# Linear attention, then a noisy top-2 mixture of experts: two key decays issued later, and another order of work at the border to expert 0

## The chip, the cores and the metric

One core of a Trainium2 chip runs the whole kernel in one launch. The metric is the device time of a run in microseconds (us), from start to end; lower is better. The engines are named as the profile names them: PE (matrix products and transposes), ACT (activations and copies), DVE (vector operations), POOL (GpSimd, which also issues indirect DMAs), SP (DMA issues).

## The reference

The first part is linear attention with a decay per head (B 4, H 8, S 768, D 64), the second a mixture of 8 experts with noisy top-2 routing over 3072 tokens of width 512 (hidden width 1024). Cut to what matters:

```python
for b in range(nb):                                   # attention
    intra = einsum('bhic,bhjc->bhij', qb, kb) * Dmask[None]
    intra = einsum('bhij,bhjd->bhid', intra, vb)
    inter = einsum('bhid,bhde->bhie', qb * lam_pow[None], kv_state)
    out[:, :, sl] = intra + inter
    kb_dec = kb * rev_pow[None]
    kv_state = lam_block * kv_state + einsum('bhsd,bhse->bhde', kb_dec, vb)
noisy_logits = x @ w_gate + log1p(exp(x @ w_noise)) * noise     # x: the attention's output
top2 = argpartition(-noisy_logits, 2, axis=1)[:, :2]            # softmax over the two
for e in range(E):
    for k in range(2):
        h = maximum(x[mask] @ w1[e], 0.0)
        out[mask] += top2_w[mask, k, None] * (h @ w2[e])
```

## The kernel before

**Attention** runs in 12 stages `t` (loop from L937) of two chunks of 128 positions each, over all 8 heads. A stage has, in this order: the gate's products of the stage before (`products`, L416), the turning of that stage's output into rows (`turn_x`, L428), the transposes of the next stage's keys and queries (L312, L325), the state update (`kv`, L400), the decayed keys of the stage after next (`kdecay(t + 2)`, L340, 8 ACT operations), the stage's own sums (`intra`, `inter(t, 0)`, L368), the copy of the two accumulators to memory on ACT (`evac_o`, L388), the logits of the stage before (L447), the scores of the next stage (`scores`, L355 on PE, L358 on DVE), and the second half of `inter`. An engine runs its own instructions in the order in which this code records them; there is no other scheduler. The accumulators `pO` and `pKV` exist once, so the second half of `inter` for the next stage can't start before `evac_o` has read them. Keys arrive by a DMA on SP's queue, which also carries the weight loads of expert 0; a load whose buffer is still read waits there, and what stands behind it waits too.

**Routing** is cut into three groups of chunks (8, 8 and 8). For each group a generator records DVE steps one by one, whenever `advance(n)` is called: `gate` (L457 to L498: logits to noisy top-2, last result `ob`), `weights`, `count` (PE, L532 to L537: how many tokens stand before each one), then `route` (DVE, L548 to L572: positions, and the one-hot tables `hot` and `rest`), and after a break called "step" 24 small products that find expert 0's tokens (L583) and the DVE chain behind them (L586 to L612). `finish(n)` drives a group to its end. The lists of tokens per expert go to DRAM by scatters on POOL (L622, one of about 1 us for each chunk and choice; `scatter` issues them at once, `paced` one by one, each behind a one-element copy L670 that waits for the named tile). `gather_rows` (L813) fetches token rows by indirect DMA.

**The border** (L992 to L1016) is what stands between the last stage and expert 0's loop: `products(11)`, the transposes of the first two gathered tiles (`trans_rows`, L822 on PE, L824 on ACT, L825 on DVE), `logits(11)`, the first two of the eight column blocks f of expert 0 (`mm1`, 12 products each, L860; `head`), and their evacuation (`evac1`, L866 on ACT, L870 on DVE). PE's results rotate through 4 buffers `pS`, which `mm1`, `turn_x` and `trans_rows` share, so the block f = 2 needs the buffer of `head[0]`.

**Expert 0** (L1018 on) runs in three parts of 2, 2 and 3 tiles: the first layer (8 blocks f, L860), then for each tile the second layer (`gemm2`, 24 products, L898). Tiles 2 and 3 come from the second group, tiles 4 to 6 from the third. The third part ends with the reading of the scattered lists (`load_rec`), the gathers of expert 1's rows and their transposes (L822). Weights are split into a high part (ACT, L771) and a low part (L775, a difference of two tensors in SBUF, on DVE or POOL).

Of the kernel before, what the change touches and what calls it, by code (L numbers as in the profile page):

```python
# [56 lines left out]
MAXOV = 40  # L57
MAXT = 24
FILLA, FILLB, FILLC = {4: 24, 5: 24, 6: 20, 7: 20, 8: 19, 9: 19, NST - 1: 24}, 2, 4
FILL1, FILL2 = 4, 9  # L60
LOADS = {2: [(1, 0)], 3: [(1, 1)], 4: [(1, 2)], 5: [(1, 3)], 9: [(2, 0), (2, 1)], 10: [(2, 2)], 11: [(2, 3)]}
HIGH = {4: [(1, 0)], 5: [(1, 1)], 6: [(1, 2)], 7: [(1, 3)], 10: [(2, 0), (2, 1)]}
LOW = {5: [(1, 0)], 6: [(1, 1)], 7: [(1, 2)], 10: [(2, 0)]}
ZEROS = {11: 8}
MID = 16
X1 = ((), (), (), (), (0, 1), (2, 3, 4), (5, 6))
WARM = (10, 1, 1)
# [20 lines left out]
def sub(ap, offset, dims):  # L88
    return bass.AP(tensor=ap.tensor, offset=ap.offset + offset, ap=dims)
# [27 lines left out]
def kernel(  # L117
# [216 lines left out]
    def kdecay(u):  # L334
        if u >= NST:
            return
        KD[u] = aw.tile([128, 2, H, D], FT, name="kd", bufs=1)
        if u > 1:
            for h in range(H):
                nc.scalar.activation(KD[u][:, :, h, :], KT[u][:, :, h, :], AF.Copy, scale=kdc[:, h, :])  # L340
            return
        for a in range(2):
            kd, kt = [x[u][:, a].rearrange("p (h s) d -> p s h d", s=2) for x in (KD, KT)]
            nc.gpsimd.tensor_mul(kd, kt, kdc.rearrange("p (h s) d -> p s h d", s=2).to_broadcast([128, 2, HP, D]))
# [40 lines left out]
    def evac_o(u):  # L385
        XO[u] = aw.tile([128, 2 * DB * C], FT, name="xo", bufs=1).rearrange("p (a d i) -> p a d i", a=2, d=DB)
        for a in range(2):
            nc.scalar.activation(XO[u][:, a], PO[u][a], AF.Copy)  # L388
# [23 lines left out]
    def products(u):  # L412

        p = psum.tile([128, 2, C], FT, name="pR")
        for d in range(DB):
            nc.tensor.matmul(p[d * 32:(d + 1) * 32], wgn[:, d, :], XO[u][:, :, d, :], start=True, stop=True)  # L416
        XP[u] = aw.tile([128, 2, C], FT, name="xp", bufs=1)
        nc.scalar.activation(XP[u], p, AF.Copy)
# [3 lines left out]
    def turn_x(u):  # L422

        XC[u] = aw.tile([128, 2, DB, C], FT, name="xc")
        for a in range(2):
            p = bank()
            for d in range(DB):
                nc.tensor.transpose(p[:, d, :], XO[u][:, a, d, :], identf)  # L428
            nc.scalar.activation(XC[u][:, a], p, AF.Copy)

    def store_x(u):

        queue = nc.gpsimd if u < NST - 4 else nc.sync
        queue.dma_start(x_tok[2 * u * C:2 * (u + 1) * C, :].rearrange("(a p) m -> p a m", a=2),
                          XC[u].rearrange("p a d i -> p a (d i)"))
# [232 lines left out]
    def paced(n, tile):  # L668
        if scatters:
            nc.gpsimd.tensor_copy(spacer, tile[0:1, 0:1])  # L670
            scatter(n)
# [101 lines left out]
    def split_low(which, e, j, half=None, low=nc.vector):  # L773
        st, hi, lo = split_parts(which, e, j, half)
        low.tensor_tensor(lo, st, hi.bitcast(FT), op=SUB)  # L775
# [42 lines left out]
    def trans_rows(t, n):  # L818

        p = psum.tile([128, DB, n], FT, name="pS", bufs=4)  # L820
        for d in range(DB):
            nc.tensor.transpose(p[:, d, :], XG[t][:n, d * 128:(d + 1) * 128], identf[:n, :n])  # L822
        hi, lo = [xt(i, slice(t * TS, t * TS + n)) for i in range(2)]
        nc.scalar.activation(hi, p, AF.Copy)  # L824
        nc.vector.tensor_tensor(lo, p, hi.bitcast(FT), op=SUB)  # L825
# [111 lines left out]
    for t in range(NST):  # L937
        u = t + 1
        if t:
            products(t - 1)  # L940
            turn_x(t - 1)
            if t == 8:
                split_low(1, 0, 3, low=nc.gpsimd)
        if u < NST:
            trans_k(u)
        load(t + 3, "kt")
        if u < NST:
            trans_q(u)
        load(t + 3, "qt")
        if u < NST:  # L950
            kv(u)
        if t:
            store_x(t - 1)
            paced(1, XC[t - 1][:, 1, 0, :])
        kdecay(t + 2)
        if u == NST:
            scatter(1)
        if u == NST:
            logits(t - 1)
        intra(t)  # L960
        load(t + 3, "vt")
        inter(t, 0)
        evac_o(t)
        paced(1, XO[t][:, 1, 0, :])
        if t and u < NST:
            logits(t - 1)
        if 2 * t in GB[1:]:
            if 2 * t > GB[1]:
                finish(GB.index(2 * t) - 2, False)
            jobs.append(routing(GB.index(2 * t) - 1))  # L970
        advance(FILLB)
        if u < NST:
            scores(u)
            inter(u, 1)
        for which, j in HIGH.get(t, []):
            split_high(which, 0, j)
        if u < NST:
            if LOW.get(t):
                nc.gpsimd.tensor_copy(spacer, AT[u][0][0:1, 0, 0, 0, 0:1])
            for which, j in LOW.get(t, []):  # L980
                split_low(which, 0, j, low=nc.gpsimd)
            paced(1, AT[u][1][:, 1, 0, 0, :])
        advance(FILLA.get(t, 18))
        for which, j in LOADS.get(t, []):
            load_w(which, 0, j)
        zero_out(ZEROS.get(t, 0))
        if t == 2:
            turn_noise()
        if t == 4:
            for i in range(4):  # L990
                nc.sync.dma_start(sub(lst, i * 128 * LI * RW, [[LI * RW, 128], [1, LI * RW]]), linit)
    products(NST - 1)  # L992
    for j in range(2):
        trans_rows(j, TS)
    logits(NST - 1)
    head = [mm1(0, 0, PARTS0[0], 0)]
    turn_x(NST - 1)
    store_x(NST - 1)
    head.append(mm1(0, 0, PARTS0[0], 1))
    att.close()  # L1000
    hp = ctx.enter_context(tc.tile_pool(name="hp", bufs=1, reuse_waits="tile"))
    HT.append(hp.tile([128, FB, 2 * CAP], FR, name="ht"))
    for t in range(NT):
        if t >= len(XG):
            XG.append(hp.tile([128, DM], FT, name=f"xg{t}"))
        PV.append(hp.tile([128, DM], FT, name=f"pv{t}"))
    split_low(2, 0, 1)
    for f in range(2):
        evac1(0, 0, PARTS0[0], f, head[f])
    scatter(sum(job[0] == 0 for job in scatters))  # L1010
    load_rec(0, 0)
    finish(1, False)
    for t in range(2, 4):
        gather_rows(0, t, GB[2] * C)
    scatter(1)
    jobs.append(routing(NG - 1))  # L1016

    for i, (t0, n) in enumerate(parts(0)):  # L1018
        for f in range(FB):
            if i or f >= 2:  # L1020
                gemm1(0, t0, n, f)
            if i == 0:
                if 1 <= f < 5:
                    split_w(2, 0, 2 + (f > 2), (f - 1) % 2)
                if f == 2:
                    nc.scalar.activation(XG[6], zero, AF.Copy)
                advance(FILL1)
            if i == 1 and f < 4:
                advance(FILL2)
                if f == 3:  # L1030
                    finish(2, False)
            if i or f >= 2:
                paced(1 + (i == 2), ht(0, 0, f, columns(0, t0, n)).bitcast(FT))
            if i == 1 and f == 2:
                load_rec(0, 1)
            if i == 2 and f == 2:
                load_rec(1, 0)
                load_rec(0, 2)
                load_rec(0, 3)
                for j in range(1, 3):  # L1040
                    load_rec(1, j)
                for t in range(NT):
                    gather_rows(1, t)
            if i == 2 and f >= 4:
                for j in X1[f - 4]:
                    trans_rows(j, size(1, j))
        if i == 0:
            zero_out(NTOK // 128)
            advance(50)
        if i == 1:  # L1050
            which_expert(1, nc.sync)
            which_list(1, nc.sync)
            for j in range(4):
                load_w(1, 1, j)
        if i == 2:
            for t in range(t0):
                scatter_out(0, t, PV[t])
        for t in range(t0, t0 + n):
            if i < 2:
                paced(3, PV[t - 1] if t > t0 else ht(0, 0, FB - 1, columns(0, t0, n)).bitcast(FT))  # L1060
            gemm2(0, t)
            if t == 0:
                advance(50)
            for j in {0: (2, 3), 2: (4, 5, 6)}.get(t, ()):
                trans_rows(j, size(0, j))
            if i == 2:
                scatter_out(0, t, PV[t][:size(0, t), :])
            if i == 2:
                for j in range((0, 2, 4)[t - t0], (2, 4, 4)[t - t0]):
                    split_w(1, 1, j)  # L1070
                    load_w(2, 1, j)
                for j in X1[t]:
                    trans_rows(j, size(1, j))
# [180 lines left out]
```

## Time and profile before

| | before |
|---|---|
| median of 3 runs | 722.18 us (721.09 to 722.67) |
| the profiled execution (its span; the slowest core is the only one) | 732.3 us |
| PE busy | 705.6 us (96%) |
| DVE / ACT / POOL busy | 356.6 / 237.9 / 291.0 us (49 / 32 / 40%) |
| mean granted TensorE clock | 0.983 |
| chain that ended last, by engine | PE 74%; issue 6%; DVE 6%; DMA 6%; SPq 2%; ACT 2%; POOL 2% |
| HBM | read 87.15 MB, written 35.55 MB, 168 GB/s over the span |

The profiled execution is a run of its own beside the three, 10.1 us longer than their median. The page's first part gives each engine's busy time; the second cuts the span into 40 slices, and its clock row shows three slices at 0.8, all others at 0.9 (the slices are 18.3 us long; those at 0.8 begin at 0, 92 and 146 us); the fourth follows the chain that ended last back through its waits. Line numbers are those of the kernel before; in the changed kernel the lines behind L60 stand one or more lower.

### The profile page before, as it was taken

What the parts mean: (1) busy time and instruction counts of PE and PEld (TensorE: products, weight loads), DVE (VectorE), ACT (ScalarE), POOL (GpSimd) and SP (SyncE); (2) the same over time, 40 slices, a digit from 0 to 9 for tenths busy, and PEclk for the clock granted to TensorE, in tenths of its full rate; (3) what the DMA queues carried; (4) which work ended last, traced back from release to release, by engine and by line L of the source; (5) the groups of instructions that cost most, each with busy time, mean ns of one, the idle gap of its engine ahead of it and who ended that gap; (6) DMA issues with size and microseconds to landing.
All of it is one profiled execution on the core that took longest, in us unless ns stands there. A gap on an engine that the chain in (4) does not pass through costs nothing.

```text
span 732.3 us, 13486 instructions
## 1 busy us (share of the span) xinstructions
PE 705.6 (96%) x4909; PEld 602.5 (82%) x4909; DVE 356.6 (49%) x808; ACT 237.9 (32%) x451; POOL 291.0 (40%) x454
## 2 busy tenths in 40 slices
PE   7999989798998999999999999999999999999996
PEld 5888878697896798798879887988888898889885
DVE  6446948677424556464436443634453444435211
ACT  1677756331121423042214230423132332214100
POOL 6110545567847354524163406233412433221311
PEclk8999989989999999999999999999999999999999
DMA  9999998673516556856365637565465556540211
GB/s 204 216 234 228 244 232 216 184 255 78 120 19 217 186 161 187 256 151 187 122 231 161 188 101 248 153 187 194 145 176 159 192 184 188 165 147 14 79 43 38
DMA packets 137658, 122.50 MB, mean 167 GB/s; under 512 B 87642, under 2 KB 106458, under 8 KB 137588
## 3 DMA queue, kind: packets, MB, share of 16 engines
q1 hardware_dynamic: 122660, 80.50, 41.2%
q0 software_dynamic: 14512, 40.57, 17.5%
q8 instruction: 40, 0.66, 0.4%
q10 hardware_dynamic: 416, 0.53, 0.2%
q14 instruction: 30, 0.25, 0.1%
HBM read 87.15 MB, written 35.55 MB: 168 GB/s over the span
## 4 chain that ended last, share of the span: by engine, by line
PE 74%; issue 6%; DVE 6%; DMA 6%; SPq 2%; ACT 2%; POOL 2%; another core or an unknown queue 1%; POOLq 0%; ACTq 0%; DVEq 0%
PE pS L860 34%; PE pKV L898 14%; PE pO L898 13%; PE pS L355 2%; SPq L153 2%; DMA kt<-in_k_dram 2%; PE pKV L368 2%; PE pO L903 2%; PE pO L368 1%; PE pS L428 1%; DMA out_dram<-ot,rec 1%; PE pKV L903 1%; ACT kd L340 1%; DMA vt<-in_v_dram 1%
## 5 line engine op out<-in xcount | busy, mean ns | idle before, releaser
L860 PE MATMUL pS<-xtl,w1h 128*128 128x512 f32 (+3 forms) x544 | 181.3, 333 | 1.7 <-DVE xtl L825 1.6
L860 PE MATMUL pS<-xth,w1h 128*128 128x512 f32 (+3 forms) x544 | 181.6, 334 | 1.1 <-DVE xtl L825 1.0
L860 PE MATMUL pS<-xth,w1l 128*128 128x512 f32 (+3 forms) x544 | 181.0, 333 | 0.0
L866 ACT ACTIVATE ht<-pS 128x512 fp32r<-128x512 f32 (+3 forms) x136 | 65.1, 483 | 220.4 <-PE pS L860 154.0
L870 DVE SCALAR_TENSOR_TENSOR ht<-pS,ht 128x256 fp32r<-128x256 f32 (+3 forms) x176 | 76.0, 453 | 110.7 <-ACT ht L866 99.8
L898 PE MATMUL pKV<-w2h,ht 128*128 128x512 f32 x384 | 124.2, 395 | 0.1
L898 PE MATMUL pO<-w2h,ht 128*128 128x512 f32 x384 | 122.7, 391 | 0.0
L860 PEld LDWEIGHTS pS<-xtl,w1h 128*128 128x128 f32 x544 | 103.3, 190 | 11.3 <-DVE xtl L825 2.3
L860 PEld LDWEIGHTS pS<-xth,w1h 128*128 128x128 f32 x544 | 103.2, 190 | 10.5 <-DVE xtl L825 1.2
L917 POOL DMA_INDIRECT out_dram<-ot,rec x46 | 62.8, 1364 | 121.3 <-DVE ot L910 108.5
L860 PEld LDWEIGHTS pS<-xth,w1l 128*128 128x128 f32 x544 | 103.3, 190 | 8.7
L898 PEld LDWEIGHTS pKV<-w2h,ht 128*128 128x128 f32 x384 | 72.9, 190 | 17.0 <-DVE ot L910 0.5
L898 PEld LDWEIGHTS pO<-w2h,ht 128*128 128x128 f32 x384 | 72.1, 188 | 16.1
L813 POOL DMA_INDIRECT xg<-x_tok,rec x46 | 51.6, 1123 | 62.5 <-DMA rec<-lst 46.8
L898 PE MATMUL pKV<-w2l,ht 128*128 128x512 f32 x192 | 76.2, 397 | 0.0
L898 PE MATMUL pO<-w2l,ht 128*128 128x512 f32 x192 | 75.4, 393 | 0.0
L882 POOL DMA_INDIRECT pv<-out_dram,rec x46 | 47.8, 1040 | 28.3 <-issue 28.3
L622 POOL DMA_INDIRECT lst<-recs,dest x48 | 48.7, 1014 | 11.1 <-issue 9.3
L1168 POOL COPY spacer<-ht 1x1 f32<-1x1 f32 x53 | 9.4, 177 | 103.4 <-ACT ht L866 103.3
L910 DVE SCALAR_TENSOR_TENSOR ot<-pKV,rec,pv 128x512 f32<-128x512 f32 x21 | 15.8, 751 | 63.0 <-PE pKV L898 43.3
L846 ACT ACTIVATE xth<-xg 128x512 fp32r<-128x512 f32 (+1 forms) x39 | 22.4, 599 | 72.1 <-DMA xg<-turned 71.9
L910 DVE SCALAR_TENSOR_TENSOR ot<-pO,rec,pv 128x512 f32<-128x512 f32 x21 | 15.8, 750 | 61.3 <-PE pO L898 47.0
(229 smaller groups left out, 950.4 us busy)
## 6 DMA issues: line engine op xcount, KB each, us to landing
wst<-in_moe_w_dram SPq DMA_DIRECT2D x48, 512.0 KB
turned<-ot SPq DMA_DIRECT2D x36, 256.0 KB
xg<-turned SPq DMA_DIRECT2D x144, 64.0 KB
wst<-in_moe_w_dram SPq DMA_DIRECT2D x32, 256.0 KB
kt<-in_k_dram SPq DMA_DIRECT2D x24, 256.0 KB
qt<-in_q_dram SPq DMA_DIRECT2D x24, 256.0 KB
vt<-in_v_dram SPq DMA_DIRECT2D x24, 256.0 KB
x_tok<-xc POOLq DMA_DIRECT2D x8, 512.0 KB
```

The source lines that it names most:

```text
L368: nc.tensor.matmul(PO[u][a][half(g), hp, :], lhs, rhs, start=n == 1, stop=n == (8 if u % NW or a else 4))
L622: st = nc.gpsimd.indirect_dma_start(out=lst, out_offset=bass.IndirectOffsetOnAxis(ap=r["dest"][:, i, c:c + 1], axis=0), in_=r["rec"][:, c, ...
L813: nc.gpsimd.indirect_dma_start(out=XG[t][:size(e, t)], out_offset=None, in_=x_tok[:rows, :], in_offset=bass.IndirectOffsetOnAxis(ap=at, ax ...
L846: nc.scalar.activation(hi, p, AF.Copy)
L860: nc.tensor.matmul(p, W1[a][d][:, fs], xt(b, cs)[:, d], start=(d == 0 and i == 0), stop=(d == DB - 1 and i == 2))
L866: nc.scalar.activation(ht(e, 0, f, cs), p, AF.Relu)
L870: nc.vector.scalar_tensor_tensor(ht(e, 1, f, c), p[:, r], 0.0, ht(e, 0, f, c).bitcast(FT), op0=OP.max, op1=SUB)
L882: nc.gpsimd.indirect_dma_start(out=PV[t][:size(e, t), :], out_offset=None, in_=out, in_offset=bass.IndirectOffsetOnAxis(ap=REC[e, t][:, 0: ...
L898: nc.tensor.matmul(p, ht(e, a, f, cs), W2[b][f // 2][:, f % 2, :], start=(i == 0), stop=(i == len(terms) - 1))
L903: nc.tensor.matmul(p[:2 * n, :], HT[0][:, f, FULL:FULL + 2 * n], W2[b][f // 2][:, f % 2, :], start=(i == 0), stop=(i == 2 * FB - 1))
L910: nc.vector.scalar_tensor_tensor(o, p, w, pv, op0=MULT, op1=ADD)
L917: st = nc.gpsimd.indirect_dma_start(out=out, out_offset=bass.IndirectOffsetOnAxis(ap=REC[e, t][:, 0:1], axis=0), in_=o, in_offset=None, bo ...
```

## The change

Three things are recorded at other places; no operation of PE is added or removed.

1. **Late key decays.** In stages 6 and 7 `kdecay(t + 2)` is recorded behind `evac_o(t)` instead of ahead of `intra(t)`.
2. **The border's order.** The transposes of tiles 0 and 1 move into the last stage, behind `turn_x(10)`. `finish(1)` (the small products and the chain of the second group) moves ahead of `head[0]`, and `products(11)`, `turn_x(11)`, `logits(11)` stand behind `head[0]`. The third group's routing starts right behind `logits(11)`, with 12 gate steps ahead of `head[1]`'s evacuation and 5 behind each block f (4 before). So `count` stands behind f = 5 on PE; before it stood behind the first `gemm2`.
3. **Weight splits and loads.** The low parts of w2's blocks 1 and 2 move from DVE (one operation of 1024 columns, two of 512) to POOL (two of 1024); block 2's high part is one ACT operation. Blocks 3's halves stay on DVE, at f = 3 and 4. `advance(50)` stands behind the transposes of tiles 2 and 3 rather than ahead of them. Two calls of `scatter` ahead of `load_rec` make explicit what was already the order.

```diff
-FILL1, FILL2 = 4, 9
+FILL0, FILL1, FILL2 = 12, 5, 9
+LATE = (6, 7)
 ...
             turn_x(t - 1)
+            if u == NST:
+                for j in range(2):
+                    trans_rows(j, TS)
 ...
-        kdecay(t + 2)
+        if t not in LATE:
+            kdecay(t + 2)
 ...
         evac_o(t)
+        if t in LATE:
+            kdecay(t + 2)
 ...
+    finish(1, False)
+    head = [mm1(0, 0, PARTS0[0], 0)]
     products(NST - 1)
-    for j in range(2):
-        trans_rows(j, TS)
+    turn_x(NST - 1)
+    split_low(2, 0, 1, low=nc.gpsimd)
     logits(NST - 1)
-    head = [mm1(0, 0, PARTS0[0], 0)]
-    turn_x(NST - 1)
     store_x(NST - 1)
+    jobs.append(routing(NG - 1))
+    advance(FILL0)
     head.append(mm1(0, 0, PARTS0[0], 1))
 ...
-    split_low(2, 0, 1)
+    for t in range(2, 4):
+        gather_rows(0, t, GB[2] * C)
+    split_high(2, 0, 2)
+    split_low(2, 0, 2, low=nc.gpsimd)
+    scatter(sum(job[0] == 0 for job in scatters))
+    load_rec(0, 0)
     for f in range(2):
         evac1(0, 0, PARTS0[0], f, head[f])
-    scatter(sum(job[0] == 0 for job in scatters))
-    load_rec(0, 0)
-    finish(1, False)
-    for t in range(2, 4):
-        gather_rows(0, t, GB[2] * C)
-    scatter(1)
-    jobs.append(routing(NG - 1))
+        advance(FILL1)
 ...
-                if 1 <= f < 5:
-                    split_w(2, 0, 2 + (f > 2), (f - 1) % 2)
+                if 3 <= f < 5:
+                    split_w(2, 0, 3, f - 3)
 ...
+            for j in {0: (2, 3), 2: (4, 5, 6)}.get(t, ()):
+                trans_rows(j, size(0, j))
             if t == 0:
                 advance(50)
-            for j in {0: (2, 3), 2: (4, 5, 6)}.get(t, ()):
-                trans_rows(j, size(0, j))
```

ACT in stage 6, before (kd are the decayed keys of stage 8, xo the evacuated outputs of stage 6, w1h a weight's high part):

```order
L328 ACTIVATE qT<-pS 128x4x128 x2
L340 ACTIVATE kd<-kt,pwt 128x2x64 x8
L388 ACTIVATE xo<-pO 128x512
L388 ACTIVATE xo<-pKV 128x512
L771 ACTIVATE w1h_312<-wst 128x1024
```

ACT at the same place in the changed kernel:

```order
L329 ACTIVATE qT<-pS 128x4x128 x2
L389 ACTIVATE xo<-pO 128x512
L389 ACTIVATE xo<-pKV 128x512
L341 ACTIVATE kd<-kt,pwt 128x2x64 x8
L772 ACTIVATE w1h_312<-wst 128x1024
```

The eight decays stand behind both evacuations and still ahead of the weight split; stage 7 is moved in the same way.

PE where the third group is counted, before (pO is the second layer of tile 0, ob the gate's result):

```order
L898 MATMUL pO<-w2l_325,ht 128x512
L898 MATMUL pO<-w2h_321,ht 128x512
L532 LDWEIGHTS lstrict
L532 MATMUL pL<-ob,lstrict 128x64
L534 LDWEIGHTS ones
```

PE where it is counted in the changed kernel (w1h_313 and w1l_317 end the block f = 5 of the first layer):

```order
L861 MATMUL pS<-xth_326,w1h_313 128x256
L861 MATMUL pS<-xtl_328,w1h_313 128x256
L861 MATMUL pS<-xth_326,w1l_317 128x256
L533 LDWEIGHTS lstrict
L533 MATMUL pL<-ob,lstrict 128x64
L535 LDWEIGHTS ones
```

Behind these now come f = 6, f = 7 and the whole second layer of tile 0, which stood ahead of the count before.

POOL at the border, in the changed kernel, from the first wait for the last stage's outputs (w2l are the low parts that came from DVE, xg the gathers of tiles 2 and 3):

```order
L671 COPY spacer<-xo 1x1
L622 MEMSET spacer 1x1
L623 DMA lst<-recs,dest 29696x2
L776 TENSOR_TENSOR w2l_323<-wst,w2h_319 128x1024
L814 DMA xg_2464<-x_tok,idx_187 128x512
L814 DMA xg_2466<-x_tok,idx_187 128x512
L776 TENSOR_TENSOR w2l_324<-wst,w2h_320 128x1024
L622 MEMSET spacer 1x1
L623 DMA lst<-recs,dest 29696x2
```

Before, five scatters in a row stood between that wait and the two gathers; now one does, and the other four stand behind the second low part.

## Rows read from the trace of the kernel before

**Rows 1.** The page, busy time by engine (us, share of span, instructions).
```profile
PE 705.6 (96%) x4909; PEld 602.5 (82%) x4909; DVE 356.6 (49%) x808; ACT 237.9 (32%) x451; POOL 291.0 (40%) x454
```
**Rows 2.** Windows by stage: stretch, length, busy us of each engine, granted clock, DMA share, GB/s.
```profile
99.00:110.00 11.00, 10.80 (x144) 9.46 (x148) 2.79 (x12) 6.85 (x16) 6.32 (x6) 0.69 1.09 230
...
135.00:150.00 15.00, 10.96 (x104) 9.09 (x101) 8.64 (x29) 4.14 (x9) 10.96 (x21) 0.80 0.69 212
...
215.00:235.00 20.00, 16.98 (x80) 13.84 (x80) 7.24 (x13) 5.59 (x8) 11.73 (x15) 0.91 0.53 178
```
**Rows 3.** Chain of waits, 76 to 126 us: start, length, what.
```profile
78.49 5.02 DMA kt<-in_k_dram
...
87.02 0.96 ACT w1h L771
...
88.31 7.32 DMA kt<-in_k_dram
```
**Rows 4.** Timeline of ACT, stages 6 to 8: start, length, operation, idle before and releaser.
```profile
83.61 2.45 ACT L340 ACTIVATE kd<-kt,pwt 128x128 f32<-128x128 f32 x8 [2.13 <-DMA kt<-in_k_dram]
...
95.74 2.45 ACT L340 ACTIVATE kd<-kt,pwt 128x128 f32<-128x128 f32 x8 [3.26 <-DMA kt<-in_k_dram]
...
99.04 1.05 ACT L771 ACTIVATE w1h<-wst 128x1024 fp32r<-128x1024 f32 x1
...
108.16 2.45 ACT L340 ACTIVATE kd<-kt,pwt 128x128 f32<-128x128 f32 x8 [0.55 <-PE pR L400]
```
**Rows 5.** Timeline of PE, stages 7 and 8.
```profile
94.47 0.62 PE L447 MATMUL pL<-sel,xp 128*128 128x16 f32 x4
...
99.20 0.32 PE L368 MATMUL pKV<-qTs,S 64*64 64x128 f32 x1 [2.12 <-ACT xo L388]
...
112.87 0.55 PE L368 MATMUL pKV<-qTs,S 64*64 64x128 f32 x6
```
**Rows 6.** Timeline of PE, last stage, border and first part of expert 0.
```profile
137.83 0.59 PE L447 MATMUL pL<-sel,xp 128*128 128x16 f32 x4 [1.18 <-DVE pos L566]
...
143.61 0.64 PE L416 MATMUL pR<-xo,wgn 128*32 128x256 f32 x8 [2.70 <-ACT xo L388]
144.18 1.97 PE L822 MATMUL pS<-identf,xg 128*128 128x128 f32 x8
...
151.31 0.36 PE L860 MATMUL pS<-xth,w1h 128*128 128x256 f32 x1
...
152.81 0.55 PE L583 MATMUL pL<-tokab,wst 128*128 128x2 bf16 x16
...
168.41 0.19 PE L532 MATMUL pL<-ob,lstrict 128*128 128x64 bf16 x1 [0.37 <-DVE oh L495]
...
177.10 0.38 PE L860 MATMUL pS<-xtl,w1h 128*128 128x256 f32 x1 [1.59 <-DVE xtl L825]
```
**Rows 7.** Timeline of DVE: the routing and the third group's gate.
```profile
136.38 1.09 DVE L564 TENSOR_SCALAR past<-past,base 128x8 f32<-128x8 f32 x1
...
155.36 0.28 DVE L457 COPY l<-pL 128x128 f32<-128x128 f32 x1
...
157.73 0.41 DVE L870 SCALAR_TENSOR_TENSOR ht<-pS,ht 128x256 fp32r<-128x256 f32 x1
158.06 0.67 DVE L775 TENSOR_TENSOR w2l<-wst,w2h 128x512 fp32r<-128x512 f32 x1
...
168.13 0.22 DVE L498 TENSOR_TENSOR ob<-oh 128x64 bf16<-128x64 f32 x1
...
174.47 0.23 DVE L564 TENSOR_SCALAR past<-past,base 128x8 f32<-128x8 f32 x1
```
**Rows 8.** Timeline of POOL at the border.
```profile
135.09 2.35 POOL L775 TENSOR_TENSOR w2l<-wst,w2h 128x1024 fp32r<-128x1024 f32 x1
...
154.90 1.04 POOL L813 DMA_INDIRECT xg<-x_tok,idx x1 [4.15 <-issue]
```
**Rows 9.** Timeline of PE, end of expert 0's third part.
```profile
223.98 0.66 PE L822 MATMUL pS<-identf,xg 128*128 128x128 f32 x4 [2.16 <-DMA xg<-x_tok,rec]
```

More of the change, by code (lines that the diff above doesn't have):

```diff
@@ L1034 @@
             if i == 1 and f == 2:
+                scatter(sum(job[0] < 2 for job in scatters))
                 load_rec(0, 1)
             if i == 2 and f == 2:
+                scatter(len(scatters))
                 load_rec(1, 0)
```

## Prediction, made before the changed kernel was run

> **What bounds the kernel now.** I read the busy times first, then the granted clock by stage, then the chain of waits and the timelines of the two places that the change touches. PE is busy for 705.6 of the 732.3 us [rows 1], so only 26.7 us of waiting can be won on it, and besides that what it loses at the low clock. The windows show where it does: 0.69 of full speed over 11 us, 0.80 over 15 and 0.91 over 20 [rows 2], that is 0.31 x 11 = 3.4, 0.20 x 15 = 3.0 and 0.09 x 20 = 1.8 us of work lost. Each of these stretches begins right behind a wait of PE: 2.12 us [rows 5], 2.70 [rows 6] and 2.16 [rows 9]. A wait of 1.59 us [rows 6] is followed by no such stretch. So a PE wait of over 2 us here costs itself and then 1.8 to 3.4 us more. The first such wait lies in attention and the second at the border, and the change works on both.
>
> **Late key decays.** In stages 6 and 7 ACT stood still for 2.13 and 3.26 us until the keys had landed [rows 4], with the outputs' evacuation queued behind the decays. In stage 7 PE's first half of the sums was done at 94.47, yet its second half began only at 99.20, after 2.12 us of waiting for that evacuation [rows 5]. With the decays behind, the evacuation starts at about 94.6. The keys of stage 9 land as before, so their decays still start at 95.74 and end near 98.1; their reader, the state update of stage 8, comes only behind that stage's products and transposes. The 2.12 us go, and with them, if no wait of over 2 us is left, the 3.4 us of the low clock: at most 5.5.
>
> What is late next are the keys of stage 10, since stage 8 still has its decays ahead of its evacuation. The load of a stage's keys leaves 0.3 us behind a weight split on ACT, and took 5.02 us once and 7.32 the next time [rows 3]. In stage 7 that split starts at 99.04 [rows 4]; with the new order it stands behind the decays and starts near 98.1, so the keys would land between 104.5 and 106.8. Then 2.45 us of decays, which before started at 108.16 [rows 4], and about 1 us of evacuations: PE's second half, before at 112.87 [rows 5], could start between 108.0 and 110.3 (PE itself would be there at 112.87 - 5.5 = 107.4). That wins 2.6 to 4.9 us. I take the middle, **3.8**. The ends for the range are 5.5 and 0: the three timed runs are 10.1 us shorter than the profiled execution, and in the time missing there some of these key waits may be missing too. Where the keys are in time, the new order changes nothing but the decays' place, with some tenths of ACT's queue at most.
>
> **The border: what goes.** Four waits and a low clock. (a) PE waited 2.70 us for the last outputs [rows 6]. Now the 16 and 8 small products and the first block f of expert 0 lie in it: 0.55 and 1.50 us (the 12 products from 151.31 to 152.81) [rows 6], so 2.05 are filled. (b) The 1.18 us ahead of the logits of stage 10 [rows 6] now hold the eight transposes, 1.97 us at half speed [rows 6] and so about 1.0 at full speed: 1.0. (c) With both of these short, the low clock of that stretch goes: 3.0. (d) The 1.59 us for the transposed tiles [rows 6] go, because the second tile's 24 products of the second layer now stand between the transposes and their reader. (e) The 0.37 us ahead of the count [rows 6] are replaced by a longer wait, below. The sum is 2.05 + 1.0 + 3.0 + 1.6 + 0.4 = **8.0**. The moved halves of w2's low parts cost DVE less (0.67 each, [rows 7]), which is counted in the next step. SP's order of loads is the same; only the low parts that free their buffers end elsewhere.
>
> **The border: what comes.** The count of the third group moves from behind the second layer of tile 0 to behind f = 5. It needs the gate's last result. The gate took from 155.36 to 168.35, 13.0 us [rows 7]; in that lie six evacuations of 0.41 and four halves of a low part of 0.67 [rows 7], so the gate alone is 13.0 - 2.5 - 2.7 = 7.8. In the changed order five evacuations and two halves lie in it: 7.8 + 2.1 + 1.3 = 11.2. Meanwhile PE has five blocks f (the second head and f = 2 to 5) of 1.50 us, 7.5 in all. So PE waits 11.2 - 7.5 = 3.7, with about 0.1 from the logits to the gate **3.8**. A part of it already falls ahead of f = 2, whose buffer comes free only when DVE evacuates the first head, behind 12 gate steps; that is the same time, not more. Queued behind the count on PE are f = 6, f = 7 and the second layer. Before, this gate was hidden beside six blocks f and a second layer.
>
> Second, POOL gets two operations of 2.35 us [rows 8]. In the trace a DVE operation on 8 columns took 1.09 us beside such an operation and ended with it (137.47 against 137.44), where the same line takes 0.23 alone [rows 7, 8]. So DVE steps that read only SBUF wait for POOL here, and the gate is made of them. The first low part starts ahead of the gate, and I count half of it, 1.2; the second lies wholly beside it, less one evacuation, 1.9. Sum **3.1**, with ends 0 (POOL done ahead of the gate, or in gaps) and 4.7 (both whole).
>
> Of this the Trainium skill, page "SBUF — State Buffer", section "SBUF: two separate sides", says that VectorE and GpSimd share one pair of ports, taken by whichever starts first for its whole instruction, while the other is blocked; it names DVE operations with two SBUF inputs or in a two-port mode. The trace agrees with it in the 1.09 us. By the rule alone both operations would count whole, 4.7 instead of 3.1, and the forecast would be 721.6.
>
> Third, a wait of 3.8 + 3.1 us at f = 2 and the count is well over 2 us, so the clock should fall behind it, over f = 6, f = 7 and the second layer. The price is the mean of the three stretches, (3.4 + 3.0 + 1.8) / 3 = **2.7**, with ends 0 and 3.4. The border gives -8.0 + 3.8 + 3.1 + 2.7 = **+1.6**.
>
> POOL's 4.7 us more are covered by the 4.15 us in which it stood still ahead of the gathers of tiles 2 and 3 [rows 8]; those 4.15 were a wait for what now comes earlier. Without that cover the lists come 0.6 us later, and the wait at 223.98 [rows 9] is where it would be paid.
>
> **Sum.** -3.8 + 1.6 = -2.2. Against the profiled execution that is 732.3 to 730.1; carried over to the median, 722.18 to **720.0**. A difference under 0.2%, about 1.4 us, can't be told from none.
>
> **Rivals.**
> 1. *The last gate is the bound and nothing pays for it.* Place: the count on PE. Price: +1.6, up to 3.8 + 4.7 + 3.4 - 8.0 = +3.9 with both POOL operations whole and the longest low clock. It decides as soon as the late decays win less than the border costs, under 1.6 us. For it: the timed runs are shorter, and the stretch with the key waits ran with its DMA engines full [rows 2], the kind of time that can be missing there. Against: 10.1 us are less than a third of what PE waits and loses to the clock in the profiled execution (26.7 + 3.4 + 3.0 + 1.8 = 34.9), so most of these waits should stand in the timed runs too. Time: 723.8 to 726.1.
> 2. *No blocking.* DVE and POOL find gaps, as the gate's PSUM readers do: 720.0 - 3.1 = 716.9, and with no fall of the clock 714.2. Against it stands the 1.09 us.
> 3. *The shift stops at the end of expert 0.* The third part ends on scattered lists, their reading and the gathers, with a wait of 2.16 us for them [rows 9]. If POOL is later by the uncovered 0.6, what PE wins ahead is waited for there: 722 to 722.8, no difference.
>
> **How the numbers follow.** The forecast has 0.38 (718.5 to 721.5, by the flight of the keys and by how much of the POOL operations counts), rival 1 0.28, rival 2 0.18, rival 3 0.16. The range that holds 8 in 10 goes from rival 2 without a fall of the clock to rival 1 with its whole price: 714.5 to 726.0. Faster: two thirds to three quarters of the forecast (0.27) and rival 2 (0.18), 0.45. Within 0.2%: the rest of the forecast and nearly all of rival 3, 0.27. Slower: rival 1, 0.28.
>
> **What would show it.** ACT's decays in stages 6 and 7 behind both evacuations, no wait of PE for xo there, and full clock from 99 to 110; a wait of ACT for the keys in stage 8 that sets how much is won. At the border, no wait over 1 us for xo; a wait of PE at f = 2 and at the count of 4 to 9 us in all, DVE steps of about 2 us beside POOL's low parts, and half clock behind the count. Wrong would be: the keys of stage 8 and 9 still waited for by PE, or a count without a wait of PE ahead of it (then rival 2), or PE's wait for the gathered rows grown by what was won ahead (rival 3).

## The result, and the profile after

The changed kernel takes 730.84 us (median of 14 runs, 724.32 to 734.29), the kernel before 723.36 us (14 runs, 721.09 to 728.98). The ratio is 1.0088, with a 95% interval of 1.0063 to 1.0113: slower by 0.9%, where 720.0 us and a gain were forecast. Medians and ranges here are of all runs, while each ratio leaves out the few runs more than 1.5% above the fastest of their kernel and so isn't the quotient of the medians. Yet the profiled execution of the changed kernel spans 727.3 us, 5.0 less than that of the kernel before. Both can't be typical. Each timed run of the study has its own span, 1.7 to 2.0 us under its time (727.3 for 729.15, 713.4 for 715.24). By that, the first profiled execution of the kernel before, of 732.3 us, was a run of about 734.1. It stands some 12 us above the median of its three runs, and not the 10.1 us that came of setting a span beside a time. The longest of 119 timed runs of that kernel in this study took 730.89.

In the trace the change does what it says. The windows of the changed kernel (stretch, length, busy us of PE, PEld, DVE, ACT and POOL, granted clock, DMA share, GB/s):

```profile
99.00:110.00 11.00, 11.00 (x168) 9.76 (x167) 6.43 (x23) 7.41 (x20) 9.06 (x14) 1.00 1.10 260
...
135.00:150.00 15.00, 11.80 (x103) 10.38 (x100) 10.05 (x38) 6.05 (x12) 11.33 (x14) 0.89 0.76 241
150.00:165.00 15.00, 9.84 (x68) 9.17 (x67) 11.85 (x55) 2.06 (x5) 10.38 (x22) 0.77 0.72 245
```

The low clock of [rows 2] from 99 to 110 us is gone; a new one, 0.77, stands at 150 to 165, where PE is busy for only 9.84 of 15 us. Timeline of ACT in stages 7 and 8 of the changed kernel:

```profile
94.09 0.60 ACT L389 ACTIVATE xo<-pO 128x512 f32<-128x512 f32 x1 [2.17 <-PE pKV L369]
...
95.06 2.44 ACT L341 ACTIVATE kd<-kt,pwt 128x128 f32<-128x128 f32 x8
...
102.50 2.45 ACT L341 ACTIVATE kd<-kt,pwt 128x128 f32<-128x128 f32 x8 [0.32 <-PE pR L401]
```

The evacuation comes first, PE no longer waits for it ([rows 5] had 2.12 us), and no decay waits for keys any more, not even that of stage 8. Timeline of PE at the border and in the first blocks f of the changed kernel:

```profile
148.69 0.39 PE L861 MATMUL pS<-xth,w1h 128*128 128x256 f32 x1 [2.31 <-DVE ht L871]
...
157.09 0.21 PE L533 MATMUL pL<-ob,lstrict 128*128 128x64 bf16 x1 [5.17 <-DVE ob L499]
...
157.59 0.56 PE L861 MATMUL pS<-xth,w1h 128*128 128x256 f32 x1
...
162.34 0.40 PE L899 MATMUL pO<-w2h,ht 128*128 128x512 f32 x1
```

Here is the new bound: 2.31 us at the block f = 4 (its buffer is the first head's, which DVE evacuates late) and 5.17 us at the count, where [rows 6] had 0.37. Behind it the 24 products of f = 6 and 7 take 4.75 us in place of 2.9. DVE and POOL say why the gate is late:

```profile
142.01 0.29 DVE L458 COPY l<-pL 128x128 f32<-128x128 f32 x1 [3.39 <-PE pL L448]
...
143.84 3.80 DVE L111 SCALAR_TENSOR_TENSOR gacc<-gacc,gu 128x64 f32<-128x64 f32 x4
```

```profile
139.44 2.36 POOL L776 TENSOR_TENSOR w2l<-wst,w2h 128x1024 fp32r<-128x1024 f32 x1
...
144.37 2.41 POOL L776 TENSOR_TENSOR w2l<-wst,w2h 128x1024 fp32r<-128x1024 f32 x1
```

Four gate steps that otherwise take 1.0 us end in 3.80, beside the second of POOL's low parts; by the single records one of the four took 3.02 us. The first low part (139.44 to 141.80) held nothing up in this execution: DVE stood idle then, waiting 3.39 us for the logits.

### The profile page after: what moved, and what is told of

Same layout as the page of the kernel before. It is cut to its first block, busy times and chain, and to the rows that moved or that the text cites. A ratio compares the mean times of both kernels' runs of the same rounds, so it can differ in the third digit from the quotient of the medians.

```text
span 727.3 us, 13483 instructions
## 1 busy us (share of the span) xinstructions
PE 702.0 (97%) x4909; PEld 598.9 (82%) x4909; DVE 357.6 (49%) x805; ACT 237.4 (33%) x450; POOL 292.7 (40%) x456
## 4 chain that ended last, share of the span: by engine, by line
PE 82%; issue 5%; DVE 4%; DMA 4%; POOL 2%; POOLq 1%; SPq 1%; ACT 1%; DVEq 0%; ACTq 0%
PE pS L861 35%; PE pKV L899 14%; PE pO L899 14%; PE pS L356 3%; PE pKV L369 2%; PE pO L369 2%; PE pS L429 2%; PE pO L904 2%; POOLq L1184 1%; PE pS L313 1%; PE pS L326 1%; PE pKV L904 1%; PE pR L417 1%; PE pS L401 1%; DMA out_dram<-ot,rec 1%
## 5 line engine op out<-in xcount | busy, mean ns | idle before, releaser
L918 POOL DMA_INDIRECT out_dram<-ot,rec x46 | 59.6, 1297 | 122.2 <-DVE ot L911 105.3
L814 POOL DMA_INDIRECT xg<-x_tok,rec x46 | 53.6, 1165 | 60.3 <-DMA rec<-lst 23.8
L883 POOL DMA_INDIRECT pv<-out_dram,rec x46 | 47.1, 1024 | 26.8 <-issue 26.8
L623 POOL DMA_INDIRECT lst<-recs,dest x48 | 48.3, 1006 | 12.2 <-issue 10.1
L1178 POOL COPY spacer<-ht 1x1 f32<-1x1 f32 x53 | 10.3, 195 | 105.9 <-ACT ht L867 105.9
```

The costliest lines, as they stand in the source:

```text
L623: st = nc.gpsimd.indirect_dma_start(out=lst, out_offset=bass.IndirectOffsetOnAxis(ap=r["dest"][:, i, c:c + 1], axis=0), in_=r["rec"][:, c, ...
L814: nc.gpsimd.indirect_dma_start(out=XG[t][:size(e, t)], out_offset=None, in_=x_tok[:rows, :], in_offset=bass.IndirectOffsetOnAxis(ap=at, ax ...
L883: nc.gpsimd.indirect_dma_start(out=PV[t][:size(e, t), :], out_offset=None, in_=out, in_offset=bass.IndirectOffsetOnAxis(ap=REC[e, t][:, 0: ...
L918: st = nc.gpsimd.indirect_dma_start(out=out, out_offset=bass.IndirectOffsetOnAxis(ap=REC[e, t][:, 0:1], axis=0), in_=o, in_offset=None, bo ...
```

## The experiments

**The kernel before once more, each half of the change alone, and the low parts back on DVE.** These four ran together; the kernel before took 715.2 us beside them (23 runs). So all times of this sitting are some 8 us lower than those above, and only the ratios are compared.

Unchanged kernel before (no edit):

> The kernel before, unchanged, for a second profile. Theory A (its first profiled execution, span 732.3 us, was an unusually long one and its median runs lack what the change removes): the span is 720 to 723, PE's wait for xo in stage 7 (2.12 us there) is under 1 us, and at least two of the three stretches at a low clock are gone. Theory B (the profile was typical and the changed kernel is slow for another reason): the waits of 2.12 and 2.70 us and the low clock behind them stand again, and the span is 728 or more.

Measured: 715.54 us, span of the profiled execution 713.4. Its windows:

```profile
80.00:99.00 19.00, 19.00 (x331) 16.45 (x330) 17.78 (x54) 13.90 (x34) 7.83 (x9) 1.00 1.13 243
99.00:110.00 11.00, 11.00 (x169) 9.76 (x168) 6.44 (x23) 7.89 (x20) 9.11 (x14) 1.00 1.11 257
...
124.00:135.00 11.00, 9.66 (x160) 7.94 (x156) 9.69 (x29) 4.49 (x8) 6.71 (x13) 1.00 0.31 81
135.00:150.00 15.00, 13.06 (x126) 12.27 (x127) 9.31 (x35) 8.06 (x18) 10.96 (x19) 1.00 0.75 238
150.00:165.00 15.00, 14.82 (x95) 12.65 (x94) 13.87 (x61) 2.21 (x5) 12.80 (x28) 1.00 0.87 279
...
215.00:235.00 20.00, 20.00 (x99) 16.53 (x98) 12.14 (x16) 7.33 (x12) 13.31 (x24) 1.00 0.73 245
```

its decays on ACT in stages 6 and 7:

```profile
81.79 2.45 ACT L340 ACTIVATE kd<-kt,pwt 128x128 f32<-128x128 f32 x8 [0.28 <-ACT qT L328]
...
91.72 2.46 ACT L340 ACTIVATE kd<-kt,pwt 128x128 f32<-128x128 f32 x8
```

and its waits of PE at the border:

```profile
131.77 0.59 PE L447 MATMUL pL<-sel,xp 128*128 128x16 f32 x4 [1.19 <-DVE pos L566]
...
136.10 0.64 PE L416 MATMUL pR<-xo,wgn 128*32 128x256 f32 x8 [1.25 <-ACT xo L388]
...
158.49 0.19 PE L532 MATMUL pL<-ob,lstrict 128*128 128x64 bf16 x1 [0.18 <-DVE ob L498]
...
183.26 1.43 PE L822 MATMUL pS<-identf,xg 128*128 128x128 f32 x12
```

Theory A holds, though the span is 7 us below the one that it named: the whole sitting is faster. The decays of stages 6 and 7 don't wait for keys, PE waits for nothing from 80 to 110 us, the clock is full in every window shown, the wait for the last outputs is 1.25 us and not 2.70, and the waits at the border sum to 1.34 + 1.94 + 0.18 = 3.5 us (length less PE's busy time in the three windows). What the change was made to remove is hardly there in this execution, and it is an ordinary one of its sitting (715.24 us against a median of 715.54). The kernel before was not traced again in a sitting where it takes 723 us, as it did beside the result; the nearest trace to that is the kernel before with two low parts on POOL, below.

The late decays alone:

```diff
+LATE = (6, 7)
 ...
-        kdecay(t + 2)
+        if t not in LATE:
+            kdecay(t + 2)
 ...
         evac_o(t)
+        if t in LATE:
+            kdecay(t + 2)
```

> The late key decays alone, in the order of before at the border. Theory A: nothing to win in the runs of the median, 722 to 724 us, the same as before within 1.5. Theory B (late decays win as they did in the profile, and the border costs more than that): 717 to 720. Theory C (the late decays themselves cost, because the state update of the next stage now waits for them): 725 or more, with a wait of PE at the state update (L400) of stages 7 and 8.

Measured: 715.42 us, ratio 0.9994 (0.9977 to 1.0010). In the median they cost nothing and win nothing here. But the profiled execution, at 717.29 us 1.9 above that median, has late keys, now in stages 8 and 9. Timelines of ACT and PE, and the window:

```profile
103.11 2.44 ACT L341 ACTIVATE kd<-kt,pwt 128x128 f32<-128x128 f32 x8 [0.99 <-DMA kt<-in_k_dram]
...
115.72 2.45 ACT L341 ACTIVATE kd<-kt,pwt 128x128 f32<-128x128 f32 x8 [3.72 <-DMA kt<-in_k_dram]
```

```profile
119.18 0.32 PE L369 MATMUL pKV<-qTs,S 64*64 64x128 f32 x1 [2.13 <-ACT xo L389]
```

```profile
110.00:124.00 14.00, 11.87 (x162) 10.07 (x160) 11.88 (x53) 7.45 (x19) 6.55 (x15) 0.88 0.78 201
```

The decays of stage 9 wait 3.72 us for their keys, PE waits 2.13 us for the evacuation behind them, and the clock falls. So late keys do come in single executions, and the new order of stages 6 and 7 leaves the same wait open two stages on. Whether it moved the wait there isn't shown.

The border alone (the changed kernel with `LATE = ()`):

> The changed kernel with the key decays where they were before. Theory A (the whole loss is the border's): 728 to 731 us, as long as the changed kernel, with 7 to 8 us of waits of PE at the fourth or fifth block f and the count, and half clock behind them. Theory C (the decays cost): 722 to 725.

Measured: 723.33 us, ratio 1.0121 (1.0101 to 1.0142), with 5.21 us of waiting at the count. The whole loss is the border's.

The low parts of w2's blocks 1 and 2 back on DVE, at the same places:

```diff
-    split_low(2, 0, 1, low=nc.gpsimd)
+    split_low(2, 0, 1)
 ...
-    split_low(2, 0, 2, low=nc.gpsimd)
+    split_low(2, 0, 2)
```

> The changed kernel with both moved low parts on DVE at the same two places. If POOL's blocking of DVE is what makes the gate long (3 to 4 us in four steps of the profile): the gate is about 0.5 us shorter (2.4 us of blocking less 1.2 of its own operation that now lies in it, twice over at most), so 729 to 731, near the changed kernel, and no DVE step of the gate takes over 0.5 us. If the blocking is what counts and the operations on DVE lie beside waits: 726 to 728.

Measured: 719.23 us, ratio 1.0077 (1.0050 to 1.0105). By the medians that is 4.1 us less than the border alone in the same sitting (which lacks the late decays, worth nothing there), by the ratios 0.44%, or 3.1 us. So POOL's blocking is a third to a half of the loss, as the second expectation had it and more than the first gave it. Timeline of PE:

```profile
143.81 0.39 PE L861 MATMUL pS<-xth,w1h 128*128 128x256 f32 x1 [0.25 <-DVE ht L871]
...
152.21 0.21 PE L533 MATMUL pL<-ob,lstrict 128*128 128x64 bf16 x1 [5.15 <-DVE ob L499]
```

The wait at f = 4 has gone, that at the count stays as long as it was: gate and products both come earlier by the same amount. The rest hangs on the count's place.

**The count's place, and what the filling is worth.** Four kernels in a second sitting, the kernel before at 715.12 us (25 runs). The count behind tile 0's second layer again:

```diff
-FILL0, FILL1, FILL2 = 12, 5, 9
+FILL0, FILL1, FILL2 = 12, 3, 9
 ...
+            if t == 0:
+                advance(50)
             for j in {0: (2, 3), 2: (4, 5, 6)}.get(t, ()):
                 trans_rows(j, size(0, j))
-            if t == 0:
-                advance(50)
```

> The changed kernel with 3 gate steps behind each block f in place of 5, and the long advance ahead of the transposes again, so that the third group's count stands behind tile 0's second layer as before; the late decays and POOL's low parts stay. If the wait of PE for the gate (5.2 us at the count) and the low clock behind it are the loss: both gone, and the time within 1.5 us of before or under it. If POOL's blocking costs PE in another way too (the buffers of the blocks f come free later): 2 to 4 us above before, with waits at blocks f of 1 to 3 us.

Measured: 718.22 us, ratio 1.0050 (1.0028 to 1.0071). Timeline of PE, and the window behind:

```profile
147.76 0.39 PE L861 MATMUL pS<-xth,w1h 128*128 128x256 f32 x1 [2.32 <-DVE ht L871]
```

```profile
150.00:165.00 15.00, 14.64 (x98) 12.55 (x97) 11.64 (x53) 2.64 (x6) 12.32 (x29) 1.00 0.84 264
```

No wait at the count, no low clock; what is left are the wait at f = 4 and 1.71 us ahead of the logits, and with the low parts on DVE, in the next kernel, only 0.40 us of the two is left. So the second expectation holds, with 3.1 us above before: the blocking costs PE through the buffers too.

Both undone, the late count and the low parts on DVE:

> The same, with the two low parts on DVE as well. If the two causes add up (count 4 us, POOL's blocking 4 us): 0 to 2.5 us below before, since the wait for the last outputs (1.25 us in the second profile of before) and the 1.2 us ahead of the logits are filled. If the filling is worth nothing: equal to before within 0.7.

Measured: 714.0 us, ratio 0.9987 (0.9972 to 1.0001), 10.3 us less than the changed kernel beside it. Its only waits of PE over 0.35 us at the border:

```profile
147.39 0.39 PE L861 MATMUL pS<-xth,w1h 128*128 128x256 f32 x1 [0.40 <-DVE ht L871]
```

The kernel before with only PE's order at the border changed:

```diff
             turn_x(t - 1)
+            if u == NST:
+                for j in range(2):
+                    trans_rows(j, TS)
 ...
+    finish(1, False)
+    head = [mm1(0, 0, PARTS0[0], 0)]
     products(NST - 1)
-    for j in range(2):
-        trans_rows(j, TS)
+    turn_x(NST - 1)
     logits(NST - 1)
-    head = [mm1(0, 0, PARTS0[0], 0)]
-    turn_x(NST - 1)
 ...
-    finish(1, False)
```

> The kernel before with only the order of PE changed at the border: transposes of tiles 0 and 1 in the last stage, the second group's small products and the first block f ahead of the last products; gate, splits and decays as before. If these fillings are real gains: 1.5 to 2.5 us below before, with no wait of PE over 0.6 us between 130 and 150 us. If the work only moves its wait (the second head then waits for its buffer, or the gate's later steps arrive later): equal within 0.7.

Measured: 715.07 us, ratio 1.0004 (0.9986 to 1.0022), scattered from 712.4 to 720.0. The profiled execution is the shortest of the twelve: 712.4 us, span 710.6, with PE busy through the whole stretch:

```profile
135.00:150.00 15.00, 15.00 (x143) 14.30 (x140) 12.79 (x52) 8.10 (x18) 11.79 (x22) 1.00 0.91 267
150.00:165.00 15.00, 15.00 (x115) 12.87 (x114) 11.94 (x56) 1.47 (x3) 12.82 (x26) 1.00 0.79 248
```

The fillings work in that execution, but the median doesn't show it.

The changed kernel once more:

> The changed kernel, unchanged, beside the others on their chip, with a second profile. Expected is the same ratio to before as first measured, 1.006 to 1.012; in the profile a wait of about 5 us at the count, and a clock under 1.0 in the windows behind it.

Measured: 724.32 us, ratio 1.0122 (1.0098 to 1.0145). Its windows at the border and its timeline of PE:

```profile
124.00:135.00 11.00, 10.68 (x175) 9.02 (x172) 9.85 (x26) 5.42 (x9) 6.68 (x13) 1.00 0.33 93
135.00:150.00 15.00, 10.97 (x108) 9.93 (x105) 12.96 (x41) 6.28 (x14) 12.60 (x16) 1.00 0.74 232
150.00:165.00 15.00, 9.79 (x66) 9.06 (x66) 11.28 (x52) 1.74 (x5) 9.41 (x22) 0.77 0.84 267
```

```profile
140.64 0.59 PE L448 MATMUL pL<-sel,xp 128*128 128x16 f32 x4 [1.71 <-ACT w2h L772]
...
147.95 0.38 PE L861 MATMUL pS<-xth,w1h 128*128 128x256 f32 x1 [2.32 <-DVE ht L871]
...
156.40 0.21 PE L533 MATMUL pL<-ob,lstrict 128*128 128x64 bf16 x1 [5.21 <-DVE ob L499]
...
156.89 0.56 PE L861 MATMUL pS<-xth,w1h 128*128 128x256 f32 x1
...
161.38 0.39 PE L899 MATMUL pO<-w2h,ht 128*128 128x512 f32 x1
...
191.19 1.42 PE L823 MATMUL pS<-identf,xg 128*128 128x128 f32 x12
...
290.32 0.50 PE L899 MATMUL pKV<-w2h,ht 128*128 128x512 f32 x1 [1.93 <-DVE ot L911]
```

This and the unchanged kernel before are two ordinary executions of the 715 us sittings, and they nearly close the sum. PE's idle time at the border is 0.32 + 4.03 + 5.21 = 9.6 us against 3.5: 6.1 more. The 24 products from 156.89 to 161.38 take 4.5 us, 1.6 more than at full clock. Together 7.7, and the transposes of tiles 4 to 6 begin at 191.19 against 183.26, 7.9 later. The rest of the 9.9 us between the spans (723.3 against 713.4) lies in expert 1, where 1.93 us of waiting stand before a second layer. The first profile of the changed kernel has such a wait too (1.70 us); the one trace of the border alone and the two of the kernel before have none. DVE's `ot` waits there for rows of the output gathered behind a scatter. Why it is late there was not tried further; as the border alone and the whole change have the same ratio (1.0121 and 1.0122), it isn't shown to come of the late decays. DVE and POOL in this execution:

```profile
137.83 2.52 DVE L607 SCALAR_TENSOR_TENSOR dest<-ei,pp 128x16 int32<-128x16 f32 x1
...
142.35 3.02 DVE L102 TENSOR_SCALAR gn<-gn 128x64 f32<-128x64 f32 x1
```

```profile
137.95 2.36 POOL L776 TENSOR_TENSOR w2l<-wst,w2h 128x1024 fp32r<-128x1024 f32 x1
...
142.89 2.41 POOL L776 TENSOR_TENSOR w2l<-wst,w2h 128x1024 fp32r<-128x1024 f32 x1
```

Two single steps, of 0.2 us each elsewhere, end with POOL's two operations (140.35 and 140.31, 145.37 and 145.30). The first holds up not the gate but the second group's chain ahead of it, and so the logits, which write to the buffer pL that the last steps of this chain read until 140.49: the 1.71 us at 140.64. The trace puts these down to an ACT operation that ends at about the same time. But with the low parts on DVE the logits don't wait, and that ACT operation starts only behind them.

**Does filling and late decays together pay?** A third sitting, with the kernel before at 723.56 us (23 runs). The first kernel is the fill-only one with `LATE = (6, 7)`:

> The order of PE at the border as in the fill-only kernel, with the late key decays of the change as well. If the fill-only kernel's scattered times (712.4 to 720.0) come from runs in which the keys of stages 8 to 10 land late, the late decays take most of these away: median 712.5 to 714, its own runs within 3 us. If they come from something else: median 714 to 715.5 with the same scatter.

Measured: 725.68 us (722.81 to 735.17), ratio 1.0016 (0.9981 to 1.0052). In this sitting the kernel before scatters as widely (721.28 to 730.89). The late decays lower neither the scatter nor the median here, so nothing speaks for late keys as the cause. For the sitting with 712.4 to 720.0 it stays untested.

The second is the fill-only kernel again:

> The fill-only kernel once more, for a second set of runs. If its gain of 2.8 us in the profile (710.6 against 713.4) is what it is worth: median 712 to 713.5. If its first median (equal to before) is: 714.5 to 715.5.

Measured: 725.23 us (723.00 to 734.01), ratio 1.0010 (0.9979 to 1.0041). Neither expectation is met by its us, since the whole sitting is slower; by its ratio the second is: no gain. Here PE stands still at the border with no wait that the trace can name, in the middle of a block of products:

```profile
147.70 0.28 PE L861 MATMUL pS<-xtl,w1h 128*128 128x256 f32 x1 [1.06 <-issue]
```

**POOL's low parts in the kernel before, and the best version again.** A fourth sitting, the kernel before at 723.29 us (23 runs).

```diff
-    split_low(2, 0, 1)
+    split_low(2, 0, 1, low=nc.gpsimd)
 ...
-                    split_w(2, 0, 2 + (f > 2), (f - 1) % 2)
+                    split_w(2, 0, 2 + (f > 2), (f - 1) % 2, nc.gpsimd if f < 3 else nc.vector)
```

> The kernel before with only the low parts of w2's blocks 1 and 2 on POOL, everything else in its order: the count stands behind the second layer of tile 0, where PE waited 0.2 us. If POOL's blocking costs by itself: the two halves of block 2 hold the gate up by some 2.4 us, less the 1.2 that DVE no longer does, so a wait of 1 to 1.5 us at the count and a time 1 to 2 us above before. If it costs only where the gate is exposed: equal to before within 0.7, though single DVE steps of the gate take over 1 us.

Measured: 726.75 us, ratio 1.0043 (1.0013 to 1.0073), 3.5 us above before by the medians. Timelines of PE, DVE and POOL, and a window:

```profile
138.53 0.64 PE L416 MATMUL pR<-xo,wgn 128*32 128x256 f32 x8 [2.62 <-ACT xo L388]
...
156.82 0.39 PE L860 MATMUL pS<-xth,w1h 128*128 128x256 f32 x1 [2.59 <-DVE ht L870]
```

```profile
152.39 4.04 DVE L110 SCALAR_TENSOR_TENSOR gacc<-gacc,gu 128x64 f32<-128x64 f32 x4
```

```profile
153.57 2.50 POOL L775 TENSOR_TENSOR w2l<-wst,w2h 128x512 fp32r<-128x512 f32 x2
```

```profile
135.00:150.00 15.00, 11.55 (x128) 10.34 (x125) 4.75 (x21) 5.99 (x13) 9.34 (x16) 1.00 0.63 214
```

It costs by itself, as the first theory said, but more than that said and at another place than either expected: nothing over 0.35 us at the count, 2.59 us at a block f, with a clock of 0.89 from 150 to 165 us. DVE's evacuation of a product buffer stands in the same queue behind the four steps, one of which took 3.27 us.

The trace also shows the border's order of before in a sitting where that kernel takes 723 us. PE's wait for the last outputs is 2.62 us there, as in the first profile, though with a full clock behind it; this execution took 729.74 us, 3.0 above its median. What doesn't come back is stage 7: PE is busy for 22.60 of the 23 us from 76 to 99 and throughout from 99 to 110, at a clock of 1.00.

> The best version so far (the changed kernel with a late count and both low parts on DVE) once more, for a second set of runs: if it is faster than before as its first median says, 0.9980 to 0.9995 of it; if the first set was chance, 0.9995 to 1.002.

Measured: 719.67 us, ratio 0.9947 (0.9916 to 0.9977), faster than before, and below both of the ranges expected. So the changed kernel with a late count and its low parts on DVE is ahead of the kernel before: by 0.5% in this sitting, and by 0.1%, with an interval that just reaches no difference, in the other. The changed kernel ran beside it only in that other one, 10.3 us slower. Why it gains where the fill-only kernel doesn't is open.

## Why the prediction was wrong

The sum was -2.2 us and the measured difference +7.5 between the medians. The step that failed is the last one, "carried over to the median": the gains were priced in one execution of the kernel before, a run of about 734 us by its span, with waits and low clocks that an ordinary execution has smaller or not at all. In the two ordinary executions compared above, the terms -3.8, -8.0 and +9.6 become 0, -3.5 and +11.2, which gives +7.7. That is near the +7.5 measured, but both traces are from sittings with smaller times; beside the changed kernel's, the medians differ by 9.2 us.

- **Late decays, -3.8.** The mechanism was right for that execution: [rows 5] and the low clock of [rows 2] are gone in the profile after, and even the wait that I put next (the keys of stage 10) wasn't there. In the profile of the late decays alone it was, with 0.99 us in stage 8, and one stage on with 3.72. In the ordinary execution the keys are in time, and in the medians the late decays are worth nothing: 0.9994 by themselves, and in a 723 us sitting 1.0016 with the fillings against 1.0010 without. The term is 0, the end of the range that I gave it.
- **What goes at the border, -8.0.** In the second profile of before, PE's waits there are 3.5 us in all, with no low clock. Of the 3.0 for the clock nothing was there, nor of the 1.59 for the transposed tiles, and of the 2.70 for the last outputs 1.25. The changed kernel removed the 3.5 and made others. Where the kernel before takes 723 us, the nearest trace has 2.62 for the last outputs, so there this term may be some 1.4 larger.
- **What comes, +9.6.** This was nearly right: 3.8 for the gate, 3.1 for POOL, 2.7 for the clock. Measured are 9.6 us of waits and 1.6 of low clock, 11.2. Of POOL's first operation I counted half. In the second profile it blocked a step whole, 2.3 us over its usual time, ahead of the logits, and in the first it fell into a gap of DVE and cost nothing; half was neither case. And I placed the wait for the buffer at f = 2; it is at f = 4.
- **Rival 1** named the mechanism, the place and the sign. Its price, 1.6 to 3.9, still set the 8.0 against the loss; with the 3.5 that ordinary executions hold, it would have been 11.2 - 3.5 = 7.7. My argument against it, that 10.1 us are less than a third of PE's waits and so most should stand in the timed runs, was wrong. The 10.1 is a span less a time and should be about 12, and the time missing is largely these waits and low clocks. In the three windows of [rows 2] the first execution waits and loses 15.5 us and the second 1.9, which is 13.5 of the 18.9 us between the two spans. How much of it is missing where the kernel before takes 723 us, no trace shows.
- **Rivals 2 and 3.** Of POOL's operations only the first found a gap, and in one of two profiles; the second blocked DVE in both. The wait at the end of expert 0 (1.59 us in the first profile of the changed kernel, 2.16 before) is in neither ordinary execution, where PE is busy for 20.00 and 19.98 of the 20 us from 215 to 235, so nothing was hidden in it there.

## What to carry to other kernels

Before a wait in a trace is counted as a gain, ask whether the profiled execution is an ordinary one: here it was about 11 us longer than the median, and the parts by which it was longer were for the most part the ones credited. A chain on another engine that just fits beside PE's work (PE waited 0.18 us for it before) can't have its reader moved ahead of 8 us of that work, nor lose the engine to another that blocks it. Where a queue also empties the buffers of the bound engine, a blocked step ahead in it is paid there first.

## What was not expected of the hardware

- A single short DVE step took 2.52 and 3.02 us beside POOL's 2.36 and 2.41 us, and 3.27 us, within four steps that took 4.04 in place of 1.0, beside two POOL operations of 2.50 in all. The Trainium skill, page "SBUF — State Buffer", section "SBUF: two separate sides", describes this as a lock held for the whole instruction; the three traces with POOL's low parts that are shown here agree in that the step ends with POOL's operation. Who came first they don't show: by the records the blocked steps began 0.1 to 0.7 us ahead of POOL's.
- A wait of PE isn't followed by a low clock from some length on, as I had read from four waits. In the late-count kernel and in the second profile of the changed one, 2.3 us at f = 4 were followed by no fall in the window up to 150 (1.00), and 2.62 us in the kernel before with POOL's low parts by none either. The 5.2 us at the count were followed by 0.77, and in the border alone 1.71 us ahead of the logits were by 0.62 over 142 to 144 us.
- The kernel before took 715 us in two sittings and 723 in the others, and one chip served in a sitting of either kind. In a trace of the second kind PE has waits inside the blocks of products of up to 1.06 us that the trace calls "issue"; the traces shown from the 715 us sittings have none there. What causes them was not tried.
